# Bias rows read skewed from an SBUF table instead of an HBM copy, in more and smaller transfers, and one PSUM bank for transposes used in two halves

## The chip, the cores and the metric

The kernel runs on one core of a Trainium2 chip. Its time is the device time of one execution in microseconds (us). One of the first three of the kernel before took 597.77 us. TensorE is the matmul engine, VectorE (DVE in the profile) and ScalarE (ACT) work elementwise, POOL is GpSimd, and SP is the engine that issues most of the hardware DMA queue (q1). POOL issues the software DMA queue (q0), which loads q, k, v and the weights and casts them to bfloat16.

## The reference

Attention with a relative position bias over 8 batches, 8 heads, 576 positions and head size 64, followed by a bilinear feed-forward layer (512 to 1536 to 512) over the 4608 rows:

```python
scores = q @ k.T / 8 + bias_table[bucket(|i - j|)]   # 32 buckets, all distances from 128 up share one
x = softmax(scores) @ v                              # heads side by side: 4608 x 512
out = ((x @ w_a) * (x @ w_b)) @ w_out
```

## The kernel before

Batch and two heads make one "pair" (32 of them; four pairs a batch). The kernel computes exp of the scores and then multiplies by exp of the bias, so the bias is a product on VectorE. For each head it holds a table of 1088 values, one for each distance. A pair's score tile has 128 key rows, and row p needs the table shifted by 4p elements. So a matrix `W` is made once: row p of `W` is 580 elements of the table from 4p on. A smaller matrix `Wt` is the same for the last 64 positions, the "tail" of a sequence, which is handled apart from the first 512.

```python
tab = nc.dram_tensor("bias_tab", [H, TB], BF16, kind="Internal")            # in HBM
W_sb = [wpool.tile([128, 2, NY], BF16, name=f"W{hp}") for hp in range(4)]   # NY = 580
...
nc.sync.dma_start(out=tab.ap(), in_=tab_sb[0:H, :])                         # SBUF table, one head a partition
for hp in range(H // 2):
    nc.sync.dma_start(out=W_sb[hp][:, :, :],
                      in_=bass.AP(tensor=tab, offset=2 * hp * TB,
                                  ap=[[NM, 128], [TB, 2], [1, NY]]))        # skew: NM = 4
for hh in range(2):
    nc.sync.dma_start(out=Wt_sb[64 * hh:64 * hh + 64, :, :], in_=...tab...)
```

The first batch is worked in halves of 256 queries. The order of the program is the order on each engine, so an instruction that has to wait holds up those written after it (in the timeline of before, shown further down, tail transposes that waited 1.63 and 1.52 us hold up the scores of pair 3 until 18.67 us). Its start (cut):

```python
t_qk(3); scale0(0, 0); scores0(2, 0)
t_tails0()                 # transposes of the tails of q and k: needs their load
scores0(3, 0); scale0(1, 0)
tail_keys0(); v_in(0, 0, 4); scores0(0, 1)
av(0, (0, 1)) ...          # products with v for the first 256 queries
scale0(0, 1); t_x(3, (0, 1), ACT); tail0(1)
av(0, (2, 3, 4))           # needs mul_tail(0), that is W and Wt
```

`scale0` multiplies by `W`. For the first 256 queries it needs columns 320 to 579 only. `mul_tail`, part of `scale0(p, 1)`, multiplies the tail's scores by `Wt` and `W`. The program's PSUM pools come to eight banks of 512 float32 values a partition; one (`ps_tr`) serves the transposes, the table and the tail's own scores.

The softmax here doesn't subtract the row's maximum and nothing guards it: scores larger than these inputs give would overflow.

## Time and profile before

| | before |
|---|---|
| time, fast runs | 439.6 to 441.1 us, median over the first three, the slow one among them, 441.12 |
| span of the profiled execution | 439.7 us |
| TensorE busy | 413.7 us, 94% |
| first feed-forward product | 34.5 us after the start |

The table of windows gives, for each stretch in us from the start, its length and the busy time of each engine in it with the number of instructions; then the granted TensorE clock as a share of full speed, the mean busy share of the DMA engines' queues and their GB/s.

```profile
core 0: us, PE busy (x) PEld busy (x) DVE busy (x) ACT busy (x) POOL busy (x), PEclk, DMA share, GB/s
0.00:14.00 14.00, 10.59 (x99) 4.79 (x102) 6.95 (x20) 8.61 (x12) 11.16 (x20) 1.00 0.98 143
14.00:19.00 5.00, 1.76 (x13) 1.03 (x14) 1.29 (x3) 1.69 (x2) 2.89 (x4) 0.79 1.46 216
19.00:26.00 7.00, 5.68 (x53) 3.20 (x50) 2.76 (x8) 4.79 (x5) 3.23 (x5) 0.50 1.33 201
26.00:60.00 34.00, 26.87 (x377) 19.84 (x377) 24.21 (x71) 23.70 (x47) 17.62 (x25) 0.98 1.42 179
60.00:360.00 300.00, 294.16 (x2554) 150.44 (x2592) 184.73 (x449) 192.31 (x266) 94.97 (x134) 1.00 0.84 96
```

From 60 to 360 us TensorE is busy 98% of the time; the slack is in the start. The slack and the clock dip (0.50 from 19 to 26 us) follow a wait. In the timeline a line has start, duration, engine, source line, operation, output and inputs, and in brackets the idle time before it and what ended it:

```profile
16.09 0.22 PE L287 MATMUL trz<-ident,tl_99 128*128 128x128 bf16 x1 [1.63 <-DMA tl_99<-in_q_dram]
17.83 0.91 PE L287 MATMUL trz<-ident,tl_99 128*128 128x128 bf16 x7 [1.52 <-DMA tl_99<-in_k_dram]
18.67 0.61 PE L351 MATMUL qkh_0_0_362<-QT_108,KT_112 64*128 64x256 bf16 x4
```

The tail transposes wait for the tails' load, and the scores of pair 3 (third line) stand behind them. The bias matrices, by contrast, were in time. Here is VectorE at the first multiplications for the second half of the queries, and the DMA issues with KB each and us from issue to landing:

```profile
31.30 0.68 DVE L366 TENSOR_TENSOR ath_1_0_396<-ath_1_0_396,W_88 128x1024 bf16<-128x1024 bf16 x1
31.90 0.69 DVE L366 TENSOR_TENSOR ath_1_1_398<-ath_1_1_398,W_88 128x1024 bf16<-128x1024 bf16 x1
32.50 0.18 DVE L408 TENSOR_TENSOR att_467<-att_467,Wt 128x64 bf16<-128x64 bf16 x1
```

```profile
W_88<-bias_tab SPq DMA_DIRECT2D x1, 290.0 KB, 6.7
W_91<-bias_tab SPq DMA_DIRECT2D x1, 290.0 KB, 8.8
Wt<-bias_tab SPq DMA_DIRECT2D x2, 96.0 KB, 8.8
```

No bracket on the first group: VectorE waited for nothing. `W` was issued from 6.7 to 8.2 us and had landed by 17.0 us; the two transfers into `Wt` followed at once (start, and the time that issuing took):

```profile
8.76 2.56 SPq L223 DMA_DIRECT2D Wt<-bias_tab  x2
```

### The profile page before, as it was taken

Reading aid. Unit: us, or ns where it says so; the run is one execution under the profiler, and the core shown is the slowest. Engines: PE = TensorE matmul, PEld = TensorE weight load, DVE = VectorE, ACT = ScalarE, POOL = GpSimd, SP = SyncE. Lnnn points to the kernel's source line nnn. Section 1 sums busy time; section 2 is a strip of 40 time slices with the busy share of each in tenths; the row PEclk is TensorE's granted clock in tenths of the full one; section 3 lists DMA queues with packets and bytes.
Section 4 is the critical chain, followed back from the end, with each engine's and each line's share of the span. In section 5 each row is a group of like instructions: output and inputs, shape, how many; then the busy total and the mean of one; then the engine's idle time right before and its main releaser. Section 6 shows DMA issues by size and latency. Waiting matters only on the chain.

```text
span 439.7 us, 8773 instructions
## 1 busy us (share of the span) xinstructions
PE 413.7 (94%) x3426; PEld 212.1 (48%) x3477; DVE 238.0 (54%) x578; ACT 252.6 (57%) x366; POOL 129.9 (30%) x187
## 2 busy tenths in 40 slices
PE   7578799999999999999999999999999999999995
PEld 3256565444445555555455545554555554444442
DVE  4467666656674566557655675466646651331320
ACT  5556766666665666566666665666566642322321
POOL 9554298268006900491039202400000000000000
PEclk9779999999999999999999999999999999999999
DMA  9999999999928981799069904950420002002004
GB/s 111 225 187 174 204 114 155 126 149 147 102 53 107 166 110 31 115 154 135 15 100 173 147 15 89 160 75 16 86 87 15 15 21 90 0 1 95 0 2 95
DMA packets 138506, 42.46 MB, mean 97 GB/s; under 512 B 115896, under 2 KB 133848, under 8 KB 138464
## 3 DMA queue, kind: packets, MB, share of 16 engines
q0 software_dynamic: 81264, 18.89, 50.7%
q1 hardware_dynamic: 51760, 13.54, 20.1%
q10 hardware_dynamic: 5440, 9.47, 6.6%
q8 instruction: 27, 0.44, 0.4%
q14 instruction: 15, 0.12, 0.1%
HBM read 39.18 MB, written 9.45 MB: 111 GB/s over the span
## 4 chain that ended last, share of the span: by engine, by line
PE 84%; DVE 6%; ACT 3%; issue 2%; DMA 2%; POOL 2%; ACTq 0%; DVEq 0%; POOLq 0%
DMA tl_99<-in_k_dram 2%; DVE g_140 L500 1%; POOL qn_93 L119 1%; POOL kn_95 L119 1%; PE po_2_5773 L507 1%; PE po_0_1445 L507 1%; PE po_0_4625 L507 1%; PE po_0_4003 L507 1%; PE po_0_3368 L507 1%; PE po_0_2733 L507 1%; PE po_0_2098 L507 1%; PE po_3_2879 L507 1%; PE po_3_4771 L507 1%; PE po_3_4149 L507 1%; PE po_3_2244 L507 1%
## 5 line engine op out<-in xcount | busy, mean ns | idle before, releaser
L157 POOL DMA_DIRECT2D vt_104<-in_v_dram x8 | 4.9, 627 | 65.3 <-PE av_3_2803 L446 27.9
L497 PEld LDWEIGHTS <-wb_126 128*128 128x128 bf16 x152 | 14.5, 97 | 19.0 <-issue 4.6
L487 PEld LDWEIGHTS <-wa_122 128*128 128x128 bf16 x160 | 15.1, 98 | 17.2 <-issue 2.0
L497 PEld LDWEIGHTS <-wb_125 128*128 128x128 bf16 x160 | 14.0, 97 | 18.1 <-issue 8.0
L487 PEld LDWEIGHTS <-wa_124 128*128 128x128 bf16 x144 | 13.3, 98 | 18.3 <-issue 3.2
L157 POOL DMA_DIRECT2D vt_103<-in_v_dram x8 | 5.2, 682 | 53.8 <-PE av_3_3438 L446 27.6
L487 PEld LDWEIGHTS <-wa_123 128*128 128x128 bf16 x152 | 13.2, 98 | 15.3 <-issue 3.6
L128 POOL DMA_DIRECT2D qn_93<-in_q_dram x24 | 18.3, 812 | 7.3 <-DMA wo<-in_moe_w_out_dram 5.7
L497 PEld LDWEIGHTS <-wb_127 128*128 128x128 bf16 x144 | 12.4, 97 | 16.6 <-issue 6.3
L137 POOL DMA_DIRECT2D kn_95<-in_k_dram x24 | 18.1, 794 | 3.8 <-PE pa_3_0_801 L487 1.8
L128 POOL DMA_DIRECT2D qn_94<-in_q_dram x24 | 18.3, 818 | 1.0 <-DMA vn_97<-in_v_dram 1.0
L137 POOL DMA_DIRECT2D kn_96<-in_k_dram x24 | 18.2, 811 | 0.0
L507 PEld LDWEIGHTS <-g_137 128*128 128x128 bf16 x36 | 3.5, 97 | 8.7 <-issue 6.8
L201 PE MATMUL warm<-zero_sb 128*128 128x512 bf16 x13 | 6.0, 568 | 1.3 <-DVE zero_sb L193 1.2
L119 POOL DMA_DIRECT2D vn_97<-in_v_dram x8 | 6.4, 798 | 2.4 <-DMA kn_95<-in_k_dram 1.8
L500 DVE TENSOR_TENSOR g_133<-pb_0_0_5590,ha_0_0_5588 128x512 bf16<-128x512 f32 x1 | 0.7, 692 | 11.4 <-PE pb_0_0_5590 L497 11.4
L119 POOL DMA_DIRECT2D vn_98<-in_v_dram x8 | 6.3, 786 | 1.0 <-DVE g_135 L500 0.7
L328 PEld LDWEIGHTS <-KB_116 64*128 64x128 bf16 x96 | 2.9, 94 | 7.5 <-issue 6.0
L507 PEld LDWEIGHTS <-g_133 128*128 128x128 bf16 x36 | 3.5, 98 | 4.6 <-issue 0.8
L507 PEld LDWEIGHTS <-g_139 128*128 128x128 bf16 x36 | 3.5, 98 | 4.3
L507 PEld LDWEIGHTS <-g_135 128*128 128x128 bf16 x36 | 3.5, 98 | 4.2
L507 PEld LDWEIGHTS <-g_140 128*128 128x128 bf16 x36 | 3.5, 98 | 4.2
(2992 smaller groups left out, 1532.8 us busy)
## 6 DMA issues: line engine op xcount, KB each, us to landing
vn_97<-in_v_dram POOLq DMA_DIRECT2D x8, 256.0 KB, 6.7
vn_98<-in_v_dram POOLq DMA_DIRECT2D x8, 256.0 KB, 6.4
wo<-in_moe_w_out_dram POOLq DMA_DIRECT2D x1, 1536.0 KB, 16.1
kn_95<-in_k_dram POOLq DMA_DIRECT2D x24, 64.0 KB, 4.9
qn_93<-in_q_dram POOLq DMA_DIRECT2D x24, 64.0 KB, 4.6
kn_96<-in_k_dram POOLq DMA_DIRECT2D x24, 64.0 KB, 4.5
qn_94<-in_q_dram POOLq DMA_DIRECT2D x24, 64.0 KB, 4.9
qn_93<-in_q_dram POOLq DMA_DIRECT2D x4, 128.0 KB, 4.3
```

The lines of the kernel that those rows point to most:

```text
L119: nc.gpsimd.dma_start(out=dst[:, 256 * h0:256 * h1].rearrange("p (h x) -> p h x", x=256), in_=src[b, h0:h1, 0:SM, :].rearrange("h (p t) d ...
L128: nc.gpsimd.dma_start(out=by_tile(qn[b % 2])[:, h0 // 4, t, :, :], in_=q[b, h0:h1, 128 * t:128 * t + 128, :].transpose([1, 0, 2]))
L137: nc.gpsimd.dma_start(out=by_tile(kn[b % 2])[:, h0 // 4, t, :, :], in_=k[b, h0:h1, t:SM:NM, :].transpose([1, 0, 2]))
L157: nc.gpsimd.dma_start(out=vt[b % 2][64 * hh:64 * hh + 64, :, hh, 0:Dh], in_=v[b, hh:H:2, SM:S, :].transpose([1, 0, 2]))
L201: nc.tensor.matmul(out=warm[:, :], lhsT=zero_sb[:, 0:128], rhs=zero_sb[:, :], start=True, stop=True)
L328: nc.tensor.matmul(out=ps[:, hh, :], lhsT=kT[r, t, :], rhs=qT[r, :, :], start=True, stop=True)
L487: nc.tensor.matmul(out=pa[:, 0:n], lhsT=wa_sb[df // 4][:, mc, 128 * (df % 4):128 * (df % 4) + 128], rhs=xn_sb[mc][:, 512 * c + lo:512 * c ...
L497: nc.tensor.matmul(out=pb[:, 0:n], lhsT=wb_sb[df // 4][:, mc, 128 * (df % 4):128 * (df % 4) + 128], rhs=xn_sb[mc][:, 512 * c + lo:512 * c ...
L500: nc.vector.tensor_tensor(out=g_sb[df][:, lo:lo + n], in0=pb[:, 0:n], in1=ff["ha"][:, 0:n], op=MULT)
L507: nc.tensor.matmul(out=po[:, :], lhsT=g_sb[df][:, 128 * tt:128 * tt + 128], rhs=wo_sb[:, df, :], start=(df == 0), stop=(df == NDF - 1))
```

## The change

Its intent: spare the trip of the table through HBM, give the columns needed first their own transfers, take the wait for the tails off the path to pair 3's scores, and let the bank for transposes be refilled in one half while the other is read. The diff, cut to its core (cut: memsets moved from the middle of the program to its start and from ScalarE to VectorE; the index arithmetic of the halves):

```diff
-    tps = ps_tr.tile([128, 512], FP32, tag="tr", name="tab_ps")
+    tps = ps_ff.tile([128, 512], FP32, tag="ffn", name="tab_ps")
...
+    def load_w(hp, y0, y1):
+        for hh in range(2):
+            src = tab_sb[2 * hp + hh:2 * hp + hh + 1, y0:y1]
+            nc.sync.dma_start(out=W_sb[hp][:, hh, y0:y1],
+                              in_=bass.AP(tensor=src.tensor, offset=src.offset,
+                                          ap=[src.ap[0], [NM, 128], [1, y1 - y0]]))
+
+    for hp in range(H // 2):
+        load_w(hp, 320, NY)
     nc.sync.dma_start(out=tab.ap(), in_=tab_sb[0:H, :])
     for hp in range(H // 2):
-        nc.sync.dma_start(out=W_sb[hp][:, :, :],
-                          in_=bass.AP(tensor=tab, offset=2 * hp * TB,
-                                      ap=[[NM, 128], [TB, 2], [1, NY]]))
+        load_w(hp, 0, 320)
     for hh in range(2):
         nc.sync.dma_start(out=Wt_sb[64 * hh:64 * hh + 64, :, :],   # as before
...
+    trb = ps_tr.tile([128, 1024], BF16, tag="tr", name="trb")
+    turn = [0]
+    def tr_half():
+        turn[0] ^= 1
+        return trb[:, 512 * turn[0]:512 * turn[0] + 512]
...                                          # t_q, t_k, t_tails0, qk_tail, t_x take tr_half()
-    t_tails0()
     scores0(3, 0)
     scale0(1, 0)
+    t_tails0()
     tail_keys0()
...                                          # the last pair
-            steps += [A(0, 1, 2), U, U, U, A(3, 4), U, U, U, lambda: t_x(s - 1), U, U, U]
+            steps += [A(0, 1, 2), U, U, U, A(3, 4), lambda: t_x(s - 1, (0, 1, 2)), U, U, U,
+                      lambda: t_x(s - 1, (3, 4)), U, U, U]
```

More of the change, by code (lines that the diff above doesn't have):

```diff
@@ L184, in padding @@
             nc.vector.memset(vt[i][64:128, :, 1, Dh:Dh + 1], 1.0)
+        for i in range(2):
+            nc.vector.memset(vm[i][:, :, :, Dh:Dh + 1], 1.0)
+            nc.vector.memset(XG[i][64:128, 4, :, :], 0.0)
     nc.sync.dma_start(out=bt_sb[0:NB, :], in_=bias_table)
@@ L205 @@
     nc.scalar.activation(out=eb_sb[0:NB, :], in_=bt_sb[0:NB, :], func=ACTF.Exp)
-    z = zero_sb[:, :].rearrange("p (a b c) -> p a b c", a=H // 2, b=2)
     for i in range(2):
-        nc.scalar.activation(out=tl[i][0:64, :, :, Dh:], in_=z[0:64], func=ACTF.Copy)
-        nc.scalar.activation(out=tl[i][64:128, :, :, 0:Dh], in_=z[64:128], func=ACTF.Copy)
-    tps = ps_tr.tile([128, 512], FP32, tag="tr", name="tab_ps")
+        nc.vector.memset(tl[i][0:64, :, :, Dh:], 0.0)
+        nc.vector.memset(tl[i][64:128, :, :, 0:Dh], 0.0)
+    tps = ps_ff.tile([128, 512], FP32, tag="ffn", name="tab_ps")
     nc.tensor.matmul(out=tps[0:H, 0:NR], lhsT=eb_sb[0:NB, :], rhs=oh_sb[0:NB, :],
@@ L271, in t_q @@
             return
-        ps = ps_tr.tile([128, 1024], BF16, tag="tr", name=f"trq{p}")
+        ps = tr_half()
         transposes(ps, qn, p)
@@ L275, in t_q, with t_k @@
              ps[:, 0:SM].rearrange("d (t p) -> d p t", t=NM))
-    def t_k(p, eng=None, pool=None, tag="tr"):
+    def t_k(p, eng=None, pool=None):
         if p >= NP or not early(p // 4):
             return
-        ps = (pool or ps_tr).tile([128, 1024], BF16, tag=tag, name=f"trk{p}")
+        ps = pool.tile([128, 1024], BF16, tag="ffn", name=f"trk{p}") if pool else tr_half()
         transposes(ps, kn, p)
@@ L284, in t_tails0 @@
     def t_tails0():
-        ps = ps_tr.tile([128, 1024], BF16, tag="tr", name="trz")
-        for j in range(8):
-            nc.tensor.transpose(ps[:, 128 * j:128 * j + 128], tl[0][:, j // 2, j % 2, :], ident[:, :])
-        nc.vector.tensor_copy(out=ZB[0][:, :, :, :],
-                              in_=ps[:, :].rearrange("d (h i c) -> d h i c", h=H // 2, i=2))
+        for i in range(2):
+            ps = tr_half()
+            for j in range(4):
+                nc.tensor.transpose(ps[:, 128 * j:128 * j + 128], tl[0][:, 2 * i + j // 2, j % 2, :],
+                                    ident[:, :])
+            nc.vector.tensor_copy(out=ZB[0][:, 2 * i:2 * i + 2, :, :],
+                                  in_=ps.rearrange("d (h i c) -> d h i c", h=2, i=2))
     def t_tails(b):
@@ L313, in v_in @@
     def v_in(b, h0, h1):
-        if b < 2:
-            nc.vector.memset(vm[b][:, h0:h1, :, Dh:Dh + 1], 1.0)
         nc.vector.tensor_copy(
@@ L387, in qk_tail @@
                          start=True, stop=True)
-        pt = ps_tr.tile([128, 512], FP32, tag="tr", name=f"qktt{p}")
+        pt = tr_half().bitcast(FP32)[:, 0:ST]
         for hh in range(2):
-            nc.tensor.matmul(out=pt[:, 0:ST], lhsT=z[:, 1, :], rhs=z[:, 0, ST * hh:ST * hh + ST],
+            nc.tensor.matmul(out=pt, lhsT=z[:, 1, :], rhs=z[:, 0, ST * hh:ST * hh + ST],
                              start=(hh == 0), stop=(hh == 1))
@@ L397, in ex_tail @@
         at = wrk.tile([128, ST + 1024], BF16, tag="att", name=f"att{p}")
-        nc.scalar.activation(out=at[:, 0:ST], in_=pt[:, 0:ST], func=ACTF.Exp, scale=scale)
+        nc.scalar.activation(out=at[:, 0:ST], in_=pt, func=ACTF.Exp, scale=scale)
         n = 768 if p < 4 else 1024
@@ L449, in av @@
         xg = XG[p % 2]
-        if p < 2 and jqs[0] == 0:
-            nc.vector.memset(xg[64:128, 4, :, :], 0.0)
         groups = [(jqs[0], 0, len(jqs), 128)]
@@ L472, in t_x @@
             return
-        ps = ps_tr.tile([128, 1024], BF16, tag="tr", name=f"trx{p}_{jqs[0]}")
+        ps = tr_half()
+        q0, q1 = 128 * jqs[0], min(SM, 128 * jqs[-1] + 128)
         for jq in jqs:
-            nc.tensor.transpose(ps[:, 128 * jq:128 * jq + 128], XG[p % 2][:, jq, :, :], ident[:, :])
-        q0, q1 = 128 * jqs[0], min(SM, 128 * jqs[-1] + 128)
-        copy(eng, xn_sb[hp][:, SM * b + q0:SM * b + q1], ps[:, q0:q1])
+            nc.tensor.transpose(ps[:, 128 * jq - q0:128 * jq - q0 + 128], XG[p % 2][:, jq, :, :],
+                                ident[:, :])
+        copy(eng, xn_sb[hp][:, SM * b + q0:SM * b + q1], ps[:, 0:q1 - q0])
         if jqs[-1] == 4:
-            copy(eng, xn_sb[hp][:, c0:c0 + ST], ps[:, SM:S])
+            copy(eng, xn_sb[hp][:, c0:c0 + ST], ps[:, SM - q0:S - q0])
     ff = {}
@@ L556, in t_qk @@
         t_q(p, ACT if p == 0 else None)
-        t_k(p, None, ps_ff, "ffn")
+        t_k(p, None, ps_ff)
     def scores0(p, h):
```

## The prediction

> **What bounds the kernel now.** The table of windows shows two regimes. From 60 us to 360 us TensorE is busy 294.2 of 300 us, from 360 us 74.6 of 80 us: only less TensorE work helps there, and the change leaves its instruction count alone (6956 rows). The slack is in the first 60 us (TensorE busy about 45 us). By the timeline, TensorE stops at 14.5 us and waits until 16.1 and 17.8 us for the q and k tails (the chain of waits gives this load 8.95 us), before the scores of pair 3 can start at 18.7 us. The granted clock then falls to 0.50 from 19 to 26 us, and score matmuls go from 0.38 to 0.61 us. The DMA view shows the software queue busy 99.6% of the first 30 us.
>
> **What the change does.**
> 1. The tail transposes move behind pair 3's scores, which can then start near 14 us instead of 18.7 us. With the moved memsets and the halved bank I cost this at 2 to 4 us saved, clock dip included.
> 2. The last pair's transposes are split, and steady-state tails use half a bank: under 0.5 us.
> 3. The bias tables W (4 x 290 KB) are no longer read from a copy in HBM. Before, they were issued at 6.7 to 8.2 us and landed 6.7 to 8.8 us later, by 13.4 to 17.0 us, and the first multiply by W began at 13.8 us: they were hardly late. Now 16 transfers read them from eight single partitions of SBUF: 2048 rows of 520 or 640 bytes instead of 1024 of 1160.
>
> Point 3 decides. [...] First-needed columns would land at about 11, 16, 21 and 26 us, in time, but the rest only at 32 to 50 us, and the small table Wt, last in that queue, at about 51 us or later. Before, Wt was first used at 32.5 us, and TensorE needs its product at once, in order. That would delay everything by some 15 to 25 us[...].
>
> [...]
>
> [...]
>
> **Prediction:** 454 us, 434 to 478 in 8 of 10; faster by over 2%: 0.08, within 2%: 0.27, slower: 0.65. A compromise between two outcomes, about 437 and about 460 us.
>
> **What would show it.** TensorE, VectorE and ScalarE nearly idle between about 31 and 50 us, ended by a product with W or Wt; long landing times for transfers into W and Wt; then the same 98% busy TensorE, shifted. Pair 3's scores at 14 to 15 us and no wait for tails before them would show point 1. The last 80 us unchanged shows point 2.
>
> **What would make it wrong.** Reads of one partition running near full DMA rate (W landing within 10 us of issue); queue order looser than I take it, so that Wt does not wait behind W; or slow reads blocking the engines so far that the loss exceeds 40 us.

Passages are cut from this text where it is marked. In them the author assumed a limit on reads from single partitions of SBUF, with figures that no trace of this case shows, and worked out from them how long each transfer into `W` takes. What these terms came to: landing times of 11 to 26 us for the first-needed columns, 32 to 50 us for the rest and 51 us or later for `Wt`, hence a delay of 15 to 25 us and about 460 us. Without such a limit on reads, `W` was to land by about 12 us and point 1 alone to remain, about 437 us; the author held the limit for more likely, about two in three; and the delay was to be larger if slow reads also held up the software queue.

## The result, and the profile after

Over the same rounds the changed kernel took 466.11 us (465.34 to 467.57), the kernel before 440.63 us. The ratio is 1.059, 95% interval 1.0551 to 1.0629: slower. A ratio here is the mean time of one kernel's fast runs over that of the other's in the same rounds, so it is not quite the ratio of the medians. Executions over 1.5% slower than the fastest of the same kernel are left out of the means.

The windows of the changed kernel, columns as above (cut: 60 to 86 us and the end):

```profile
0.00:14.00 14.00, 7.17 (x61) 3.06 (x64) 6.68 (x24) 4.03 (x5) 9.19 (x17) 0.82 0.84 85
14.00:19.00 5.00, 3.80 (x38) 1.74 (x38) 1.20 (x3) 1.94 (x2) 1.75 (x3) 0.50 1.29 129
19.00:26.00 7.00, 4.97 (x38) 2.15 (x36) 3.94 (x8) 5.42 (x6) 4.37 (x7) 0.73 0.79 44
26.00:60.00 34.00, 11.31 (x146) 8.40 (x144) 9.15 (x26) 7.87 (x15) 10.69 (x15) 0.60 1.23 140
86.00:386.00 300.00, 294.46 (x2544) 150.11 (x2582) 183.31 (x445) 192.59 (x266) 88.14 (x125) 1.00 0.81 93
```

The 300 us from 86 us on are the same as before's from 60 us on (294.5 against 294.2 us of TensorE). The loss lies in the start. There the DMA rate is lower, not higher: 85 and 44 GB/s where before had 143 and 201. VectorE at the lines that were shown of before:

```profile
36.13 0.69 DVE L384 TENSOR_TENSOR ath_1_0_408<-ath_1_0_408,W_88 128x1024 bf16<-128x1024 bf16 x1 [2.52 <-DMA W_88<-tab_sb]
36.74 0.69 DVE L384 TENSOR_TENSOR ath_1_1_410<-ath_1_1_410,W_88 128x1024 bf16<-128x1024 bf16 x1
55.70 0.19 DVE L426 TENSOR_TENSOR att_474<-att_474,Wt 128x64 bf16<-128x64 bf16 x1 [18.27 <-DMA Wt<-bias_tab]
```

The product with `Wt` comes at 55.70 instead of 32.50 us: 23.2 us, nearly the whole difference of the spans (463.6 - 439.7 = 23.9 us). 18.3 us of it are one wait for `Wt`, 2.5 us a wait for `W`; the other 2.4 us had been lost before. TensorE, in order, waits with VectorE (18.4 us for `att_474`). The view of waits gives waiter, what it waited for, total, times and longest:

```profile
ACT ath_1_0_609 L375 <- PE qkh_1_0_599 L369: 22.1, 1, 22.1
PE av_2_561 L460 <- DVE att_474 L433: 18.4, 1, 18.4
DVE att_474 L426 <- DMA Wt<-bias_tab: 18.3, 1, 18.3
```

Why was `Wt` late? Here are SP's DMA issues in order of time, with start and the time the issues took together (cut: the first parts of `W_91`, the table's copy to HBM, the second parts of `W_89`):

```profile
4.67 1.24 SPq L224 DMA_DIRECT2D W_88<-tab_sb  x2
5.95 4.19 SPq L224 DMA_DIRECT2D W_89<-tab_sb  x2
10.18 6.94 SPq L224 DMA_DIRECT2D W_90<-tab_sb  x2
21.11 5.18 SPq L224 DMA_DIRECT2D W_88<-tab_sb  x2
27.83 9.80 SPq L224 DMA_DIRECT2D W_90<-tab_sb  x2
37.68 7.58 SPq L224 DMA_DIRECT2D W_91<-tab_sb  x2
45.30 2.49 SPq L234 DMA_DIRECT2D Wt<-bias_tab  x2
```

`Wt` was issued only at 45.3 us, and then took 9 us more. In between SP was not waiting for a semaphore (up to 85 us it did so three times: 3.0 us ahead of the first of these issues, and twice 0.7 us). It stood in the issues themselves: single ones took 0.6 us at first and up to 7.4 us later, and the 16 into `W` took 37.9 us together. That they stood there because the transfers ahead did not move on is a reading that e1 and e2 bear out (eight issues took 18.5 us in e1's group B and 3.7 us in its E; e2's 16 took 9.8 us). The DMA view shows how long transfers took from issue to landing:

```profile
W_90<-tab_sb SPq DMA_DIRECT2D x2, 80.0 KB, 17.7
W_91<-tab_sb SPq DMA_DIRECT2D x2, 80.0 KB, 13.9
Wt<-bias_tab SPq DMA_DIRECT2D x2, 96.0 KB, 9.0
```

An 80 KB transfer took 13.9 and 17.7 us where a 290 KB one had taken 6.7 to 8.8. In 10 to 20 us the hardware queue moved 0.28 MB, in 30 to 40 us 0.29 MB: 28 to 29 GB/s.

### The profile page after: what moved, and what is told of

It is laid out like the page before. It is cut to its first block, busy times and chain, and to the rows that moved or that the text cites. A ratio compares the mean times of both kernels' runs of the same rounds, so it can differ in the third digit from the quotient of the medians.

```text
span 463.6 us, 8792 instructions
## 1 busy us (share of the span) xinstructions
PE 415.9 (90%) x3426; PEld 212.9 (46%) x3477; DVE 239.6 (52%) x582; ACT 250.4 (54%) x362; POOL 129.9 (28%) x187
## 4 chain that ended last, share of the span: by engine, by line
PE 78%; SPq 9%; DVE 4%; ACT 3%; DMA 2%; issue 2%; ACTq 0%; DVEq 0%
SPq L224 8%; DMA Wt<-bias_tab 2%; DVE g_140 L517 1%; PE po_0_1429 L524 1%; PE po_0_2708 L524 1%; PE po_0_3970 L524 1%; PE po_0_4588 L524 1%; PE po_0_3339 L524 1%; PE po_0_2077 L524 1%; PE po_3_2853 L524 1%; PE po_3_4733 L524 1%; PE po_3_4115 L524 1%; PE po_3_3484 L524 1%; PE po_3_2222 L524 1%; PE po_3_5749 L524 1%
## 5 line engine op out<-in xcount | busy, mean ns | idle before, releaser
L504 PEld LDWEIGHTS <-wa_122 128*128 128x128 bf16 x160 | 15.2, 98 | 17.5 <-issue 2.2
L514 PEld LDWEIGHTS <-wb_126 128*128 128x128 bf16 x152 | 14.5, 97 | 18.6 <-issue 4.2
L514 PEld LDWEIGHTS <-wb_125 128*128 128x128 bf16 x160 | 14.0, 97 | 18.1 <-issue 8.0
L504 PEld LDWEIGHTS <-wa_124 128*128 128x128 bf16 x144 | 13.3, 98 | 18.3 <-issue 3.4
L504 PEld LDWEIGHTS <-wa_123 128*128 128x128 bf16 x152 | 13.1, 97 | 15.3 <-issue 3.6
L128 POOL DMA_DIRECT2D qn_93<-in_q_dram x24 | 18.3, 818 | 6.6 <-DMA wo<-in_moe_w_out_dram 5.9
L514 PEld LDWEIGHTS <-wb_127 128*128 128x128 bf16 x144 | 12.4, 97 | 16.6 <-issue 6.3
L137 POOL DMA_DIRECT2D kn_95<-in_k_dram x24 | 18.1, 799 | 4.3 <-PE trb L408 2.0
L137 POOL DMA_DIRECT2D kn_96<-in_k_dram x24 | 18.2, 813 | 0.0
L460 PE MATMUL av_2_561<-vt_103,att_474 128*128 128x130 bf16 x3 | 0.8, 269 | 18.4 <-DVE att_474 L433 18.4
L375 ACT ACTIVATE ath_1_0_609<-qkh_1_0_599 128x1024 bf16<-128x1024 f32 x1 | 1.0, 1023 | 22.1 <-PE qkh_1_0_599 L369 22.1
L426 DVE TENSOR_TENSOR att_474<-att_474,Wt 128x64 bf16<-128x64 bf16 x1 | 0.2, 193 | 18.3 <-DMA Wt<-bias_tab 18.3
L460 PEld LDWEIGHTS <-att_474 128*128 128x128 bf16 x3 | 0.3, 111 | 18.6 <-DVE att_474 L433 18.6
L524 PEld LDWEIGHTS <-g_137 128*128 128x128 bf16 x36 | 3.5, 97 | 8.7 <-issue 6.8
L151 POOL DMA_DIRECT2D tl_100<-in_k_dram x8 | 5.1, 662 | 5.5 <-DMA vt_103<-in_v_dram 2.7
```

The costliest lines, as they stand in the source:

```text
L128: nc.gpsimd.dma_start(out=by_tile(qn[b % 2])[:, h0 // 4, t, :, :], in_=q[b, h0:h1, 128 * t:128 * t + 128, :].transpose([1, 0, 2]))
L137: nc.gpsimd.dma_start(out=by_tile(kn[b % 2])[:, h0 // 4, t, :, :], in_=k[b, h0:h1, t:SM:NM, :].transpose([1, 0, 2]))
L151: nc.gpsimd.dma_start(out=tl[b % 2][64 * hh:64 * hh + 64, :, i, Dh * hh:Dh * hh + Dh], in_=src[b, hh:H:2, SM:S, :].transpose([1, 0, 2]))
L460: nc.tensor.matmul(out=pav[:, slot, :, :], lhsT=weights_tail(p, jq), rhs=vt[i][:, hp, :, :], start=True, stop=True)
L504: nc.tensor.matmul(out=pa[:, 0:n], lhsT=wa_sb[df // 4][:, mc, 128 * (df % 4):128 * (df % 4) + 128], rhs=xn_sb[mc][:, 512 * c + lo:512 * c ...
L514: nc.tensor.matmul(out=pb[:, 0:n], lhsT=wb_sb[df // 4][:, mc, 128 * (df % 4):128 * (df % 4) + 128], rhs=xn_sb[mc][:, 512 * c + lo:512 * c ...
```

## The experiments

Theory (the "port theory" of the expectations): what makes the transfers slow is where in SBUF they read, all 128 rows of one from a single partition, and the eight partitions of the table side by side. This no run had shown. Rivals: the number and the small size of the rows and transfers; or other parts of the change. Kernels shared the runs of before: 439.4 us (median of 11) for e1 to e4, 438.95 us for e5 to e8.

### e1: the reads by themselves

A kernel with transfers only; a single run. Its output is wrong, which doesn't matter for the time. Each group is eight transfers of 128 rows of 640 bytes (655,360 bytes), and each waits for the group before.

```python
for j in range(8): from_parts("B", j, j, 1, 1, 4)   # one partition, row p skewed by 4p elements: as in the kernel
# A: all eight from partition 0.  C: partition 4j.  D: row p from partition p.  E: skewed from HBM.
# F: 16 partitions 0-15, 8 rows each.  G: 16 partitions 0,4,...,60.  H: partition 0, no skew.
# then eight loads of q by the POOL queue: alone, with B beside them (J), with E beside them (K)
```

> Only transfers, in groups of eight that wait for the group before; the result is wrong on purpose. Each transfer writes 128 rows of 640 bytes (82 KB, 655 KB a group). Port theory [...]: groups A (all from partition 0), B (partition j, as in the kernel), C (partition 4 j) and H (no skew) take about 24 us each; D (each row from its own partition) and E (skewed from the table in HBM) under 6 us; F [...] about 6 us and G [...] about 3 us. [...] Rival, that the number and size of rows and transfers is the cost: A to H all alike. J (Pool-queue loads beside B): [...] the loads take several times as long as alone; K (beside E) much less.

Between groups VectorE copies a few elements, so the bracket of its timeline is the time of the group that ended:

```profile
31.16 0.18 DVE L42 COPY dst_B<-dst_A 128x32 bf16<-128x32 bf16 x1 [27.00 <-DMA dst_A<-src_sb]
55.80 0.18 DVE L42 COPY dst_C<-dst_B 128x32 bf16<-128x32 bf16 x1 [24.46 <-DMA dst_B<-src_sb]
70.09 0.18 DVE L42 COPY dst_D<-dst_C 128x32 bf16<-128x32 bf16 x1 [14.11 <-DMA dst_C<-src_sb]
76.73 0.18 DVE L42 COPY dst_E<-dst_D 128x32 bf16<-128x32 bf16 x1 [6.46 <-DMA dst_D<-src_sb]
82.78 0.17 DVE L42 COPY dst_F<-dst_E 128x32 bf16<-128x32 bf16 x1 [5.88 <-DMA dst_E<-bias_tab]
92.42 0.18 DVE L42 COPY dst_G<-dst_F 128x32 bf16<-128x32 bf16 x1 [9.46 <-DMA dst_F<-src_sb]
99.23 0.18 DVE L42 COPY dst_H<-dst_G 128x32 bf16<-128x32 bf16 x1 [6.63 <-DMA dst_G<-src_sb]
125.09 0.18 DVE L42 COPY ld<-dst_H 128x32 bf16<-128x32 bf16 x1 [25.69 <-DMA dst_H<-src_sb]
134.98 0.18 DVE L42 COPY ld<-ld 128x32 bf16<-128x32 bf16 x1 [9.71 <-DMA ld<-in_q_dram]
157.28 0.18 DVE L42 COPY ld<-ld 128x32 bf16<-128x32 bf16 x1 [22.05 <-DMA ld<-in_q_dram]
173.42 0.18 DVE L97 CAST zero<-ld 128x32 f32<-128x32 bf16 x1 [11.72 <-DMA ld<-in_q_dram]
```

Same rows, same sizes, same number of transfers: A 27.0 and B 24.5 us against D 6.5 and E 5.9 us. So the form of the transfers is not the cause; where they read from is. 655,360 bytes / 24.46 us is 26.8 GB/s for B. The skew doesn't matter (H, without it, 25.7 us; A 27.0). F and G both read 16 partitions, 8 rows of each: 9.5 us with the partitions side by side, 6.6 us with every fourth (G can't show more: SP took 5.0 us to issue it). If only the number of partitions counted, they would be equal; so it counts which partitions are read. B and C say the same: both read eight partitions, one a transfer, but B's lie side by side and C's four apart (24.5 against 14.1 us).

Nor did one DMA engine do the work alone: in the windows of e1 the 16 engines were busy 0.60 of A's and of B's time on average. C is also the largest miss: it was expected at 24 us, like A and B. The sizes of others were missed too: F took 9.5 us (69 GB/s), not about 6, G 6.6 and not about 3, D 6.5 and not under 6. Slow reads also hold SP: issuing the eight transfers took 18.5 us in B and 3.7 us in E.

The last three lines answer another question. Eight loads of the POOL queue took 9.7 us alone and 22.0 us beside B; beside E they took 11.7 us. So slow reads in one queue also hold up the other queue, here by a factor of 2.3, where "several times" was expected. How the two queues hold each other up was not shown.

### e2 and e3: the table of HBM again, the rest of the change kept

e2 keeps the 16 transfers and their two parts, with `Wt` behind them, but reads the copy in HBM, which is therefore written ahead of all of them; e3 takes the four transfers of before. The diff of e2:

```diff
-            src = tab_sb[2 * hp + hh:2 * hp + hh + 1, y0:y1]
             nc.sync.dma_start(out=W_sb[hp][:, hh, y0:y1],
-                              in_=bass.AP(tensor=src.tensor, offset=src.offset,
-                                          ap=[src.ap[0], [NM, 128], [1, y1 - y0]]))
+                              in_=bass.AP(tensor=tab, offset=(2 * hp + hh) * TB + y0,
+                                          ap=[[NM, 128], [1, y1 - y0]]))
+    nc.sync.dma_start(out=tab.ap(), in_=tab_sb[0:H, :])
     for hp in range(H // 2):
         load_w(hp, 320, NY)
-    nc.sync.dma_start(out=tab.ap(), in_=tab_sb[0:H, :])
     for hp in range(H // 2):
         load_w(hp, 0, 320)                  # then Wt, as in the changed kernel
```

> The changed kernel with the same 16 transfers into W, but read from the table in HBM. Port theory: the stall of 18 us on Wt is gone, W lands within about 10 us of issue, time 435 to 442 us. Rival, number and size of transfers: stays above 458 us.

> The changed kernel with the four transfers of before into W; all else of the change kept. Port theory: 435 to 441 us; at most 1% faster than before by the reordered tails and the halved bank. Rival, that another part of the change costs time too: clearly slower than before, 445 us or more.

e2 took 437.21 us, ratio 0.9935 (0.990 to 0.997); e3 438.03 us, ratio 0.9959 (0.9935 to 0.9983). The stall is gone in both, with 16 transfers as with four. By e3 the rest of the change costs no time on balance. Both beat both kernels by a little. In e2 `Wt` still stands behind all 16 transfers, but SP has issued these within 9.8 us instead of 37.9:

```profile
8.00 9.77 SPq L223 DMA_DIRECT2D W<-bias_tab  x16
18.06 2.01 SPq L233 DMA_DIRECT2D Wt<-bias_tab  x2
```

### e4: the kernel before with nothing but the new reads

The edit is the `load_w` part of the change's diff, put into the kernel before.

> The kernel before with nothing changed but the reads of W. Port theory: all of the loss, 462 to 472 us, with TensorE idle until Wt lands near 55 us. Rival, that other parts of the change share the loss: under 458 us.

466.94 us, ratio 1.0621 (1.0589 to 1.0654), with a wait of 20.9 us for `Wt`. So the reads of `W` carry the whole loss. The changed kernel's ratio of 1.059 is a little lower, but the intervals overlap.

### e5: `Wt` ahead of the second parts of `W`

```diff
     nc.sync.dma_start(out=tab.ap(), in_=tab_sb[0:H, :])
+    for hh in range(2):                     # the two transfers into Wt, moved up
+        nc.sync.dma_start(out=Wt_sb[64 * hh:64 * hh + 64, :, :], in_=...)
     for hp in range(H // 2):
         load_w(hp, 0, 320)
-    for hh in range(2):
-        nc.sync.dma_start(out=Wt_sb[64 * hh:64 * hh + 64, :, :], in_=...)
```

> The changed kernel with the two transfers into Wt put ahead of the second parts of W; the slow reads stay. If Wt's place behind W in the one queue makes the 18 us stall, the first product with Wt moves from 55.7 us to about 37 us, and the next stall is then the second part of W for pairs 2 and 3, landing near 50 us: 452 to 457 us. If the reads stall the engines regardless of order, no gain: above 463 us.

457.52 us, ratio 1.0411, a little above the expected range. The wait for `Wt` is gone, and waits for the second parts of `W` stand in its place:

```profile
42.43 1.30 DVE L384 TENSOR_TENSOR ath<-ath,W 128x1024 bf16<-128x1024 bf16 x2 [7.94 <-DMA W<-tab_sb]
49.78 1.30 DVE L384 TENSOR_TENSOR ath<-ath,W 128x1024 bf16<-128x1024 bf16 x2 [3.08 <-DMA W<-tab_sb]
55.54 1.30 DVE L384 TENSOR_TENSOR ath<-ath,W 128x1024 bf16<-128x1024 bf16 x2 [0.88 <-DMA W<-tab_sb]
```

The first product with `Wt` came at 43.6 us, not 37: `Wt` could be issued only when the table's copy had landed (issued 20.15, `Wt` issued 30.20 us), and the second parts began after that. So `Wt`'s place was worth some 8 us (ratio 1.059 to 1.041), and the other 18 us of loss stay with the slow reads.

### e6: the same reads from partitions four apart

Heads on partitions 0, 4, ... 28 instead of 0 to 7; transfers and their order unchanged (diff cut to its core):

```diff
-    eb_sb = const.tile([128, H], BF16, name="eb_sb")
+    eb_sb = const.tile([128, 4 * H], BF16, name="eb_sb")       # zero but for every fourth column
...
-            src = tab_sb[2 * hp + hh:2 * hp + hh + 1, y0:y1]
+            h4 = 4 * (2 * hp + hh)
+            src = tab_sb[h4:h4 + 1, y0:y1]
```

> The changed kernel with the eight heads' rows of the table on partitions 0, 4, ... 28 [...] instead of 0 to 7 [...]; same transfers, same order, still one partition a transfer. Port theory, with group C of the reads alone (14.1 us against 24.4 us): W complete near 30 us, Wt near 33 us, the stall on Wt shrinks from 18 us to under 4 us: 438 to 448 us. If the single partition were the limit: as the change, 463 us or more.

444.79 us, ratio 1.0133 (1.0087 to 1.0179). `Wt` is now issued at 24.3 us, and the wait for it has shrunk from 18.3 to 3.8 us:

```profile
34.39 0.19 DVE L428 TENSOR_TENSOR att<-att,Wt 128x64 bf16<-128x64 bf16 x1 [3.81 <-DMA Wt<-bias_tab]
```

Moving eight rows of the table to other partitions gives back 21 of 25 us or so; each transfer still reads a single partition. So in the kernel itself, too, it counts which partitions are read. It remains some 7 us slower than e3 (6.8 us by the medians); 3.8 us are this wait, and the rest was not pursued. It was run at another time.

### e7 and e8: the moved tail transposes

e7 is the kernel before with `t_tails0()` moved behind `scale0(1, 0)` and nothing else. e8 is e3 with it moved back.

> The kernel before with only the tail transposes moved behind pair 3's scores. If the reorder is what the 0.4% of e3 comes from: 436 to 439 us, ratio 0.993 to 0.998. If the halved bank and the moved memsets give it: 1.000.

> e3 (changed kernel, W from HBM in four transfers) with the tail transposes back ahead of pair 3's scores. If the reorder is the gain of e3: ratio near 1.000, clock dip near 20 us back. If the halved bank and the moved memsets give it: near 0.996.

e7: 438.92 us, ratio 0.9991 (0.996 to 1.0021). e8: 439.47 us, ratio 1.0001 (0.997 to 1.0031). Neither part alone shows a gain; together, in e3, 0.4%. The intervals overlap, so how the 0.4% divides stays open. The traces show a difference all the same. In e7 TensorE waits 0.3 us for the tails instead of 3.1 us, and the clock from 19 to 26 us is 0.76 (before 0.50; e8, where the transposes stand ahead again, 0.58). In e3 it is 1.00:

```profile
14.00:19.00 5.00, 3.27 (x32) 1.44 (x31) 4.22 (x9) 4.29 (x5) 1.96 (x3) 1.00 1.41 222
19.00:26.00 7.00, 4.85 (x84) 3.36 (x83) 4.24 (x11) 4.53 (x7) 3.22 (x6) 1.00 1.33 201
```

In before the clock was 0.50 from 18 to 26 us, after TensorE had been busy for 0.8 us of the four from 14 to 18 us. In the changed kernel TensorE did nothing from 40 to 55 us, and the clock was 0.50 there and up to 60 us. What sets the clock was not shown.

### The halved bank, read from the traces

No experiment gave the halves two banks. But the traces show what the halves do. The tail transposes fill one half, VectorE copies it, and they fill the other half; e3's timeline:

```profile
16.83 0.40 PE L299 MATMUL trb<-ident,tl 128*128 128x128 bf16 x4
17.26 0.42 DVE L301 COPY ZB<-trb 128x512 bf16<-128x512 bf16 x1
17.74 0.38 PE L299 MATMUL trb<-ident,tl 128*128 128x128 bf16 x4 [0.52 <-DVE ZB L301]
```

The second half's matmuls begin at 17.74 us, just after the copy of the first half ended (17.26 + 0.42 = 17.68 us), and the profile names that copy as what they waited for (0.52 us). It is the same in the five traces looked at (0.51 to 0.56 us). So in the program as built the halves take turns like one tile, at these transposes. No run here shows what would happen without the wait.

## Why the prediction was right or wrong

The measured 466.11 us lies in the range of 434 to 478, and "slower" had the largest chance, 0.65. The range held both outcomes, so that alone says little; but the course given for the slow case, reads into `W` that are slow and `Wt` late behind them, is the one that the experiments found.

- **What bounds the kernel: right.** 300 us of the steady part have 294 us of TensorE in both kernels. All 23.9 us of the spans' difference are there by the first output product (82.8 us before, 106.75 us after).
- **Point 3, slow reads from single partitions: right in effect.** e1's group B gives 24.46 / 8 = 3.06 us for a transfer of 640-byte rows. In the changed kernel the first-needed columns landed by about 13.5, 19.4, 21.6 and 26.8 us (predicted 11, 16, 21, 26), and the second parts of pairs 0 to 2 by 36.0, 41.1 and 48.2 us (predicted 32 to 50 for all four), from issue and landing times of the trace. The three engines stood idle from about 37 to 55.7 us (predicted 31 to 50), ended by the product with `Wt`. e6 moved the table's rows to partitions four apart, and the time fell by 21 us.
- **`Wt` last in that queue: right in effect, another way in detail.** It landed near 55.6 us against "about 51 us or later". It did not wait in the queue alone; SP itself stood in its issues until 45.3 us.
- **Mis-sized: the delay of "some 15 to 25 us" and with it the slow outcome of "about 460".** Apart from the reads the change gives about 2 us (e3) and not 2 to 4, and the product with `Wt` came 23.2 us later: the upper end of the range for the delay, 466 and not 460.
- **Named only as a possibility: slow reads hold up the software queue.** They do: 9.7 to 22.0 us in e1. In the changed kernel the loads of k for the first batch took 6.6 us to land (median) against 4.3, and pair 3's scores began at 20.7 us, although no wait for tails stands before them any more. The prediction had put these scores at 14 to 15 us. That sign of point 1 failed, and e3 shows that the reads were to blame for most of it: with HBM reads they begin at 15.6 us, still a little late.
- **Point 1, "2 to 4 us saved": too much.** With the `W` reads taken out, the rest of the change gave 0.4%, 1.8 us (e3); the moved transposes alone 0.1% and not clear of zero (e7). The term that failed is counting a wait of 3 us and the slow clock after it as time of the whole kernel: removing the wait moved the first feed-forward product from 34.5 to 32.2 us in e7's profile, but its runs are not measurably shorter.
- **Point 2, the last pair and half a bank, under 0.5 us: nothing seen against it.** The last part of the two profiles (from the first output product to the end) is 356.9 us in both.

454 us was a compromise between two outcomes, and neither of the two was 454.

## What to carry to other kernels

Look at which partitions a DMA reads, and how many, as well as at the bytes: many rows from one SBUF partition at a time came at 24 to 27 GB/s (groups A, B and H of e1), the same with the eight partitions four apart at 46 GB/s (C, 655,360 bytes in 14.11 us), while rows of the same size from HBM came at about 111 GB/s (E, 655,360 bytes in 5.88 us). A detour through HBM can be the short way. And a slow transfer's price is paid by what is behind it in its queue (`Wt`, issued at 45.3 us instead of 8.8 us) and by the other queue (loads of 9.7 us took 22.0 us in e1): look for the last and smallest table in the queue, and for the other queue's landing times, before moving a load. Two halves of a PSUM bank did not work as two buffers in the tail transposes (the second waited 0.52 us for the copy of the first).
